# Decode attention with a gated side branch on one core: the last output weights in six pieces, the result in four stores

## The chip, the core and the metric

The kernel runs on one core of a Trainium2 chip. The metric is the device time of one execution in microseconds (us), the median of several runs. The core has a matrix engine (PE, with its weight loads as PEld), VectorE (DVE), ScalarE (ACT), GpSimd (POOL) and SyncE (SP). SP and ACT each issue transfers on a queue of their own; all transfers share 16 DMA engines. In the traces q1 is SP's queue and q10 is ACT's.

## The reference

One decode step for 8 sequences: layer norm of x, attention over the last 2048 keys of a cache with 8 key heads and 32 query heads, the output projection, multiplied by the SiLU of a gated feed-forward branch, plus x.

```python
x  = A_x                                   # 8 x 1 x 512
xn = _layernorm(x, axis=-1)
# _A_ref, with W = 2048, Hq = 32, Hkv = 8, Dh = 128
q = (xn @ wq).reshape(B, 1, 32, 128).transpose(0, 2, 1, 3)
k = jnp.repeat(k_cache[:, :, Sk - W:, :], 4, axis=1)
v = jnp.repeat(v_cache[:, :, Sk - W:, :], 4, axis=1)
p = softmax(einsum("bhqd,bhkd->bhqk", q, k) * 128 ** -0.5)
o = einsum("bhqk,bhkd->bhqd", p, v)
s = o.transpose(0, 2, 1, 3).reshape(B, 1, 4096) @ wo      # wo: 4096 x 512
# _B_ref
h = sigmoid(xn @ w_gate) * (xn @ w_up)
g = silu(h @ w_down)
return x + s * g                            # 8 x 1 x 512, bf16
```

Keys and values that are read are 32 MB each, the weights some 13 MB; the result is 8 KB.

## The kernel before, in words

Everything comes in through SP's queue (`q0`), but for half of `w_gate` and one small copy of x, which ACT's queue (`q1`) takes. The loads stand in one list in the order in which they are wanted (`later`, line 107). A load goes out when its buffer pool has room: there are five buffers for keys ("k") and four for values ("v"), of 2 MB each, and `pump` (line 110) issues from the head of the list only, so an entry that has no room holds back all behind it. `free` (line 116) is called where the program has used up a buffer. An issue then waits on SP for the last reader of the buffer that it takes over.

The list is: x and the feed-forward weights in value buffers (three of them), the query weights in two key buffers, sixteen key tiles (sequence b, half i of the heads) with the value tiles three places behind, and at the end the output weights `wo` in pieces (line 176, `want_rows` at 120, `load_rows` at 97). Each partition holds 32 rows of `wo` of 1 KB; a piece is rows t0 to t1 of every partition, in one buffer of a pool.

For each sequence PE turns the keys (line 421), multiplies them with the queries (440), and two sequences behind multiplies the probabilities with the values (537, in `values`, which frees a value tile after its last column). The order of the last two sequences is written out by hand from line 627 on. Then come the output products: rows 0 to 19 (`KS` is 20) of `wo` into `part_ps` (line 659), copied by ACT (669); this partial sum (line 685) and the rows 20 to 31 one by one go into `fin_ps`, four products per row at four column blocks (673, called at 686).

`fin_ps` has the four blocks of 128 output columns on partitions 0, 32, 64 and 96 and, within a block, the eight sequences four partitions apart (`Z` is 32, `S` is 4, `NB` is 4). VectorE multiplies by the gate (`prod`, line 688) and adds x (`y_bf`, line 690). Two stores write the result (line 693), one on each queue, two blocks each. x in the same layout is `x4_sb`, called x_sb in the trace; ACT loads it at line 157.

Of the kernel before, what the change touches and what calls it, by code (L numbers as in the profile page):

```python
# [10 lines left out]
def kernel(  # L11
# [14 lines left out]
    P = 128  # L26
# [54 lines left out]
    q0, q1 = nc.sync, nc.scalar  # L81
# [15 lines left out]
    def load_rows(w, tag, per, r0, r1, name):  # L97
        t = pools[tag].tile([P, r1 - r0, w.shape[1]], bf16, name=name, tag=tag)
        q0.dma_start(  # L99
            out=t[:], in_=w.rearrange("(p r) n -> p r n", r=per)[:, r0:r1, :]  # L100
        )
        return t
# [4 lines left out]
    def later(tag, f):  # L107
        todo.append((tag, f))

    def pump():  # L110
        while todo and room[todo[0][0]] > 0:
            tag, f = todo.pop(0)
            room[tag] -= 1
            f()
# [5 lines left out]
    def want_rows(name, w, tag, per, r0, r1):  # L120
        def f():
            t = load_rows(w, tag, per, r0, r1, name)
            for r in range(r0, r1):
                weights[(name, r)] = t[:, r - r0, :]

        later(tag, f)

    def want_cache(tiles, cache, tag, b, i):
        def f():
            tiles[(b, i)] = load_cache(cache, tag, b, i)  # L130

        later(tag, f)

    RT = 32
    KS = 20
# [4 lines left out]
    Z = 32  # L140
    S = Z // B
    NB = D // P
# [28 lines left out]
    for n in range(len(order) + AHEAD):  # L171
        if n < len(order):
            want_cache(k_tiles, A_k_cache, "k", *order[n])
        if n >= AHEAD:
            want_cache(v_tiles, A_v_cache, "v", *order[n - AHEAD])
    for t0, t1 in ((0, 12), (12, KS), (KS, 26), (26, 30), (30, RT)):
        want_rows("wo_sb", A_wo, "k", RT, t0, t1)

    pump()

# [7 lines left out]
        out=perm[:].rearrange("k (l p) -> k l p", l=G),  # L188
        in_=ident[:].rearrange("k (p l) -> k l p", l=G),
# [13 lines left out]
        out=rstd[:], in_=mv[:, 1:2], func=AF.Sqrt, bias=eps_t[:], scale=1.0  # L203
# [4 lines left out]
        out=xn_bf[:],  # L208
# [8 lines left out]
    for kt in range(KT):  # L217
        nc.tensor.transpose(  # L218
            out=xnT_ps[:, kt, :],
            in_=xn_bf[:].rearrange("b (p kt) -> b kt p", kt=KT)[:, kt, :],  # L220
# [11 lines left out]
    for t in p_buf:  # L232
# [7 lines left out]
        out=own_q[:], in_=ident_f[:].rearrange("k (h q) -> k q h", q=NDQ), axis=AX.X  # L240
# [3 lines left out]
        out=sel_z[:], in_=ident_f[:].rearrange("k (j z) -> k z j", z=Z), axis=AX.X  # L244
# [6 lines left out]
    def hidden(name):  # L251
# [21 lines left out]
        out=h_sb[:].rearrange("k t p -> k p t"),  # L273
# [7 lines left out]
        out=hT_sb[:].rearrange("k t z -> k (t z)"),  # L281
        in_=h_sb[:].rearrange("k t p -> k (t p)"),
# [4 lines left out]
    for t in range(FT):  # L287
        j = t % NB
# [53 lines left out]
    for x in range(Hkv // JQ):  # L342
        for r in range(rep):
            nc.tensor.transpose(
                out=qT_ps[:, x, r, :], in_=q_bf[:, x, r, :], identity=ident[:]
            )
        nc.vector.tensor_copy(
            out=qm_sb[:, :, x * JQ : (x + 1) * JQ, M0 : M0 + rep],
            in_=qT_ps[:, x].rearrange("d r (j z) -> d z j r", z=Z)[:, ::S],
# [11 lines left out]
    for i in range(NQ):  # L361
        nc.vector.tensor_copy(
            out=turn_rows[:].rearrange("k (i j l r) -> k i j l r", i=NQ, j=NJ, l=G)[
                :, i
            ],
            in_=ident[:].rearrange("k (l j i r) -> k i j l r", i=NQ, j=NJ, l=G)[:, i],
        )
        nc.vector.reduce_sum(
            out=sel_den[:, i * Hh : (i + 1) * Hh].rearrange("k (l r) -> k l r", l=G),
            in_=ident_f[:].rearrange("k (l j i r) -> k i l r j", l=G, j=NJ, i=NQ)[:, i],  # L370
            axis=AX.X,
        )
    for e in range(2):
        nc.vector.reduce_sum(
            out=sel_out[:, e, :].rearrange("k (i h) -> k i h", i=NQ),
            in_=ident_f[:].rearrange(
                "k (i m e h) -> k e i h m", i=NQ, m=NJ // 2, e=2
            )[:, e],
# [9 lines left out]
        out=sel_res[:],  # L388
# [6 lines left out]
        out=sel_sum[:], in_=sel_den[:].unsqueeze(2).to_broadcast([P, Hq, NDQ])  # L395
# [261 lines left out]
    for t in range(KS):  # L657
        j = t % NB
# [29 lines left out]
    nc.vector.tensor_tensor(out=prod[:], in0=gg_sb[:], in1=fin_ps[:], op=ALU.mult)  # L688
    y_bf = work.tile([P, P], bf16, name="y_bf")
    nc.vector.tensor_tensor(out=y_bf[:], in0=prod[:], in1=x4_sb[:], op=ALU.add)  # L690
    HP = P // 2
    for x, q in enumerate((q0, q1)):
        q.dma_start(
            out=out.flatten_outer_dims().rearrange("b (j c) -> j b c", c=P)[
                x * NB // 2 : (x + 1) * NB // 2
            ],
            in_=y_bf[x * HP : (x + 1) * HP : S, :],
        )


# [28 lines left out]
```

## Time and profile before

| | us |
|---|---|
| median of three runs (199.91 to 200.09) | 200.05 |
| the profiled execution | 200.05 |
| its span, first to last instruction | 198.1 |
| PE busy in the span | 153.7 |
| VectorE busy | 121.6 |
| ScalarE busy | 37.6 |
| last load landed, PE resumes | 194.02 |
| `y_bf` done, stores issued | 195.12 |
| mean transfer rate over the span | 411 GB/s, 81.32 MB |

The page cuts the span into 40 slices of about 5 us; a digit is the busy share of a slice in tenths, and "GB/s" what the transfer engines moved in it. The part on queues gives packets, megabytes and the share of the 16 engines' time. The chain of work that ended last is followed back from the last instruction and lists start, duration and what ran. The timeline merges like instructions of one engine: start, duration, engine, line, operation, and in brackets how long the engine had been idle and what ended that. Windows give, for a stretch, its length, the busy time and count of PE, PEld, DVE, ACT and POOL, the clock granted to PE, the share of the transfer engines and GB/s. The granted clock is 1.00 up to 191 us, 0.88 in the us from 191 and 0.50 from 192 on.

Besides these views I use the trace's records of single packets (start, duration, size, queue), which no view lists; where a number is from them it is said.

### The profile page before, as it was taken

The numbers are of one execution on the slowest core, as the hardware profiler recorded it, in microseconds if no ns is written. First come the engines' busy times: TensorE is split into PE (matmuls) and PEld (weight loads), VectorE is DVE, ScalarE is ACT, GpSimd is POOL, SyncE is SP. The second block draws the span as 40 slices with busy tenths as digits, with TensorE's granted clock in tenths as the row PEclk, the third lists the DMA queues.
The fourth block names the chain that finished last, engine by engine and source line by source line (L and its number), as shares of the span: only waits on it lengthen the run. The fifth ranks groups of instructions, "written<-read, shape, count | busy, mean of one in ns | idle before, by whom it ended". The sixth has DMA issues, their size and how long they took to land.

```text
span 198.1 us, 4749 instructions
## 1 busy us (share of the span) xinstructions
PE 153.7 (78%) x2128; PEld 103.8 (52%) x2128; DVE 121.6 (61%) x225; ACT 37.6 (19%) x91; POOL 1.4 (1%) x10
## 2 busy tenths in 40 slices
PE   0435365999799996979798959997989797888652
PEld 0101125776676574656565646675657565566421
DVE  3752025999798586748675927587858674752301
ACT  3301010001700500230024000600140033082010
POOL 2000000000000000000000000000000000000000
PEclk9999999999999999999999978999999999999985
DMA  6999999999999999999999999999999999999970
GB/s 225 436 428 430 440 430 427 430 424 428 424 447 427 424 424 427 427 430 440 430 430 422 427 427 430 433 428 437 424 424 424 433 433 427 437 420 432 410 314 14
DMA packets 6299, 81.32 MB, mean 411 GB/s; under 512 B 768, under 2 KB 776, under 8 KB 1416
## 3 DMA queue, kind: packets, MB, share of 16 engines
q1 hardware_dynamic: 6082, 80.10, 94.9%
q10 hardware_dynamic: 198, 0.93, 1.4%
q8 instruction: 16, 0.26, 0.5%
q14 instruction: 3, 0.02, 0.0%
HBM read 81.02 MB, written 0.01 MB: 409 GB/s over the span
## 4 chain that ended last, share of the span: by engine, by line
DMA 76%; PE 21%; SPq 1%; issue 0%; DVE 0%
DMA k_sb<-in_A_k_cache_dram 63%; PE kT_ps L421 12%; DMA wo_sb<-in_A_wo_dram 11%; PE o_ps L537 4%; PE s_ps L440 3%; DMA wg_sb<-in_B_w_gate_dram 2%; SPq L99 1%; PE fin_ps L673 1%; PE pT_ps L511 0%; DVE prod L688 0%; PE m_ps L475 0%; DVE y_bf L690 0%; PE m_ps L458 0%; SPq L89 0%
## 5 line engine op out<-in xcount | busy, mean ns | idle before, releaser
L426 DVE COPY kT_sb<-kT_ps 128x1024 bf16<-128x1024 bf16 x128 | 85.4, 688 | 35.7 <-PE kT_ps L421 34.9
L421 PE MATMUL kT_ps<-perm,k_sb 128*128 128x128 bf16 x1024 | 76.9, 224 | 15.0 <-DMA k_sb<-in_A_k_cache_dram 15.0
L421 PEld LDWEIGHTS <-k_sb 128*128 128x128 bf16 x1024 | 60.1, 100 | 35.2 <-DMA k_sb<-in_A_k_cache_dram 18.1
L537 PE MATMUL o_ps<-v_sb,pT_sb 128*32 128x256 bf16 x512 | 40.0, 278 | 1.2 <-DVE o_sb L558 0.9
L537 PEld LDWEIGHTS <-pT_sb 128*32 128x32 bf16 x512 | 22.1, 97 | 9.8 <-issue 3.3
L440 PE MATMUL s_ps<-kT_sb,qm_sb 128*32 128x512 bf16 x256 | 25.8, 393 | 0.7 <-DVE kT_sb L426 0.7
L488 ACT ACTIVATE p_buf<-s_ps,nb 32x512 bf16<-32x512 f32 x32 | 21.7, 678 | 0.5
L481 ACT COPY nb<-m_ps 128x1 f32<-128x1 f32 x8 | 1.3, 159 | 91.7 <-PE m_ps L475 91.7
L511 PE MATMUL pT_ps<-turn_rows,p_buf 128*128 128x128 bf16 x128 | 11.0, 230 | 1.5 <-ACT p_buf L488 1.5
L504 DVE COPY pT_sb<-pT_ps 128x1024 bf16<-128x1024 bf16 x14 | 9.6, 687 | 3.9 <-PE pT_ps L511 3.9
L511 PEld LDWEIGHTS <-p_buf 128*128 128x128 bf16 x128 | 9.4, 151 | 3.4 <-ACT p_buf L488 2.1
L440 PEld LDWEIGHTS <-qm_sb 128*32 128x32 bf16 x256 | 6.6, 93 | 7.7 <-issue 1.2
L553 ACT ACTIVATE o_odd<-o_ps,own_col 128x128 f32<-128x128 f32 x8 | 2.9, 368 | 29.0 <-PE o_ps L537 29.0
L325 PE MATMUL q_ps<-wq_sb,xnT_sb 128*32 128x512 bf16 x32 | 3.8, 627 | 4.2 <-DMA wq_sb<-in_A_wq_dram 4.2
L488 ACT ACTIVATION_READ_ACCUMULATOR p_buf<-s_ps,nb 32x1 f32 x32 | 5.9, 184 | 0.0
L455 DVE TENSOR_REDUCE st<-s_ps 128x1 f32<-128x512 f32 x8 | 5.5, 684 | 0.5 <-PE s_ps L440 0.5
L341 DVE CAST q_bf<-q_ps 128x512 bf16<-128x512 f32 x1 | 0.7, 692 | 7.4 <-PE q_ps L325 7.4
L218 PE MATMUL xnT_ps<-ident,xn_bf 8*128 8x8 bf16 x4 | 0.3, 174 | 5.6 <-DVE xn_bf L207 5.6
L580 DVE SCALAR_TENSOR_TENSOR own<-m_ps,inv,own_q 128x128 f32<-128x128 f32 x8 | 2.8, 344 | 3.1 <-PE m_ps L571 3.1
L558 DVE SCALAR_TENSOR_TENSOR o_sb<-o_ps,own_col,o_odd 128x128 f32<-128x128 f32 x8 | 2.7, 340 | 3.1 <-ACT o_odd L553 3.1
L325 PEld LDWEIGHTS <-xnT_sb 128*32 128x32 bf16 x32 | 1.1, 130 | 6.4 <-issue 4.7
L255 PE MATMUL h_ps<-wu_sb,xnT_sb 128*32 128x448 bf16 x16 | 1.7, 572 | 3.3 <-DMA wu_sb<-in_B_w_up_dram 3.3
(72 smaller groups left out, 58.3 us busy)
## 6 DMA issues: line engine op xcount, KB each, us to landing
k_sb<-in_A_k_cache_dram SPq DMA_DIRECT2D x16, 2048.0 KB, 33.4
v_sb<-in_A_v_cache_dram SPq DMA_DIRECT2D x16, 2048.0 KB, 27.1
wq_sb<-in_A_wq_dram SPq DMA_DIRECT2D x2, 2048.0 KB, 22.4
wu_sb<-in_B_w_up_dram SPq DMA_DIRECT2D x1, 1792.0 KB, 10.1
wd_sb<-in_B_w_down_dram SPq DMA_DIRECT2D x1, 1792.0 KB
wo_sb<-in_A_wo_dram SPq DMA_DIRECT2D x1, 1536.0 KB, 18.2
wo_sb<-in_A_wo_dram SPq DMA_DIRECT2D x1, 1024.0 KB
wg_sb<-in_B_w_gate_dram ACTq DMA_DIRECT2D x1, 896.0 KB, 4.6
```

The costliest lines, as they stand in the source:

```text
L325: nc.tensor.matmul(q_ps[x][Z * j : Z * (j + 1), :], lhsT=xnT_sb[:, kt, :], rhs=weights[("wq_sb", kt)][:, g * rep * Dh : (g + 1) * rep * Dh ...
L421: nc.tensor.transpose(out=kT_ps[:, c, :], in_=k_sb[:, j * CU + h * CH + c, :], identity=perm[:],)
L426: nc.vector.tensor_copy(out=kT[(b, u)][:, h * CH : (h + 1) * CH, :], in_=kT_ps[:])
L440: nc.tensor.matmul(s_ps[b][NR * l : NR * (l + 1), :], lhsT=qm_sb[:, b, i * G + l, o : o + Z], rhs=t[:, :, PG * l : PG * (l + 1)], start=(u ...
L455: nc.vector.reduce_max(out=st[b][:], in_=s_ps[b][:], axis=AX.X)
L488: nc.scalar.activation(out=p_buf[b % 2][rows, :, l, :], in_=s[rows, :].rearrange("k (c p) -> k p c", p=PG), func=AF.Exp, bias=nb[rows, :], ...
L504: copy(out=pT[b][:, h * CH : (h + 1) * CH, :], in_=pT_ps.pop(h)[:])
L511: nc.tensor.transpose(out=pT_ps[h][:, c, :], in_=p_buf[b % 2][:, :, :, h * CH + c].rearrange("k p l -> k (p l)"), identity=turn_rows[:],)
L537: nc.tensor.matmul(o_ps[rows, b % 2, :].rearrange("k (e d) -> k e d", e=2), lhsT=pT[b][:, c, rows], rhs=v[:, m, c], start=(c == 0), stop=( ...
L553: nc.scalar.mul(out=o_odd[:], in_=o_ps[:, b % 2, Dh:], mul=own_col[:, 1:2])
L558: nc.vector.scalar_tensor_tensor(out=o_of[b // 2][:, b % 2, :], in0=o_ps[:, b % 2, :Dh], scalar=own_col[:, 0:1], in1=o_odd[:], op0=ALU.mul ...
L580: nc.vector.scalar_tensor_tensor(out=own[:], in0=m_ps[:, b % 2, P : 2 * P].rearrange("p (q t) -> p q t", q=NDQ), scalar=inv[y][:, b % 2 : ...
```

## The change

Two places. The rows 20 to 31 of `wo` came in pieces of 6, 4 and 2 rows; they now come in pieces of 5, 4, 2 and 1, and the last one asks for a value buffer where the others ask for key buffers. The result was stored by one transfer of two blocks on each queue; now each block of eight rows is a transfer, blocks 0 and 2 on SP and 1 and 3 on ACT.

```diff
-    for t0, t1 in ((0, 12), (12, KS), (KS, 26), (26, 30), (30, RT)):
+    for t0, t1 in ((0, 12), (12, KS), (KS, 25), (25, 29), (29, 31)):
         want_rows("wo_sb", A_wo, "k", RT, t0, t1)
+    want_rows("wo_sb", A_wo, "v", RT, 31, RT)
```

```diff
-    HP = P // 2
-    for x, q in enumerate((q0, q1)):
-        q.dma_start(
-            out=out.flatten_outer_dims().rearrange("b (j c) -> j b c", c=P)[
-                x * NB // 2 : (x + 1) * NB // 2
-            ],
-            in_=y_bf[x * HP : (x + 1) * HP : S, :],
-        )
+    y = out.flatten_outer_dims().rearrange("b (j c) -> j b c", c=P)
+    for j in range(NB):
+        q = (q0, q1)[j % 2]
+        q.dma_start(out=y[j], in_=y_bf[Z * j : Z * (j + 1) : S, :])
```

## The prediction

> **What bounds the kernel now.** I read the page's forty slices first, then the chain of work that ended last, then the end in order of time, because the change touches only the last transfers in and the transfers out. From the page:
>
> ```profile
> DMA  6999999999999999999999999999999999999970
> GB/s 225 436 428 430 440 430 427 430 424 428 424 447 427 424 424 427 427 430 440 430 430 422 427 427 430 433 428 437 424 424 424 433 433 427 437 420 432 410 314 14
> q1 hardware_dynamic: 6082, 80.10, 94.9%
> q10 hardware_dynamic: 198, 0.93, 1.4%
> ```
>
> Apart from the first slice the transfer engines are full until some 190 us, at 410 to 447 GB/s. The bytes are the bound; the change moves the same bytes in, so only what happens around the last of them can move the time. The chain from 185 us on:
>
> ```profile
> 171.27 22.10 DMA wo_sb<-in_A_wo_dram
> 193.37 0.04 issue
> 193.41 1.04 PE fin_ps L673 x24
> 194.45 0.02 issue
> 194.47 0.30 DVE prod L688
> 194.77 0.03 issue
> 194.80 0.29 DVE y_bf L690
> ```
>
> The landing of the last output weights ends last; then come matrix products, two VectorE operations (over at 195.09) and, behind the chain, the stores. The timeline of that stretch:
>
> ```profile
> 192.17 0.83 PE L673 MATMUL fin_ps<-wo_sb,oP_sb 128*32 128x128 bf16 x24
> 193.41 1.02 PE L673 MATMUL fin_ps<-wo_sb,oP_sb 128*32 128x128 bf16 x24 [0.41 <-DMA wo_sb<-in_A_wo_dram]
> 194.02 0.14 PEld L673 LDWEIGHTS <-oP_sb 128*32 128x32 bf16 x7 [0.19 <-issue]
> 195.12 0.65 SPq L693 DMA_DIRECT2D out_dram<-y_bf  x1
> 195.12 0.61 ACTq L693 DMA_DIRECT2D out_dram<-y_bf  x1
> ```
>
> Six rows (24 products) were there at 192.17. At 193.41 PE resumes with the four rows 26 to 29, and the weight load that resumes at 194.02 belongs to rows 30 and 31, the last piece. Both stores are issued at 195.12, 0.65 us on SP and 0.61 on ACT. When they moved shows in narrow windows (the columns end with the DMA share and GB/s):
>
> ```profile
> 196.36:196.52 0.16, 0.00 (x0) 0.00 (x0) 0.00 (x0) 0.00 (x0) 0.00 (x0) 0.50 0.12 26
> 196.52:196.72 0.20, 0.00 (x0) 0.00 (x0) 0.00 (x0) 0.00 (x0) 0.00 (x0) 0.50 0.00 0
> 196.72:196.88 0.16, 0.00 (x0) 0.00 (x0) 0.00 (x0) 0.00 (x0) 0.00 (x0) 0.50 0.12 26
> ```
>
> Two bursts: by the packet records ACT's (196.37 to 196.50), then SP's (196.73 to 196.86), each at a share of 0.12, that is about 2 of 16 engines. SP sees SP's completion at 197.20; the closing barrier ends the span at 198.08. So from the stores' issue at 195.12 the path is SP's: issue 0.65, flight to the first packet 0.96, packets 0.13, completion 0.34, sum 2.08.
>
> **The last rows, 12-8-6-4-2 to 12-8-5-4-2-1.** The last piece shrinks from two rows to one, so one row's four products fewer follow the last landing. The six rows at 192.17 took 0.83 us, one product 0.31 (median for line 673), so a row adds (0.83 - 0.31) / 5 = 0.10. Saved: 0.10 us. Against it, the packets: in the packet records one of 6, 4, 2 and 1 KB takes 234, 159, 84 and 44 ns (the last in the load of x), a completion 9; 5 KB lies halfway between 4 and 6, 197. An engine moves eight packets per piece. Before: 8 x (234 + 159 + 84) + 3 x 9 = 3843 ns; after: 8 x (197 + 159 + 84 + 44) + 4 x 9 = 3908. The last landing is 0.07 us later. Together -0.03; bounds -0.10 (more packets cost nothing) and +0.07 (PE gains nothing). The middle pieces land 8 x 37 = 296 ns earlier, worth nothing: their products were never last.
>
> The one-row piece needs a value buffer. Nineteen tiles went through that pool (three weights, sixteen cache tiles) and it has four buffers, so this one takes the place of value tile (6, 0). Its last reader is among the first 16 of the 32 products that start at 176.29 and take 1.51, thus free at about 177.05. SP holds the transfer from 172.18 (end of the fifth issue) until then; behind it on SP there are only the stores, at 195. An issue of 0.44 makes it 177.5, while the same queue works off what it has until past 190. Cost nothing, covered by some 13 us; were the release later than that, each us would show fully. Transfers also take turns at eight completion semaphores and wait for the previous holder (SP's store waited for a cache tile from 172.2 to 179.4, far ahead of need). The new piece takes that of a cache tile issued at 150.05; two of the four stores take those of the first two output pieces, of which the second was in use at 190.35. None of these waits is late.
>
> **Four stores.** Now each store names two blocks of eight rows, later one block. q10's 198 packets are 144 for half of w_gate (128 data and 16 completions), 36 for x in four blocks (32 and 4) and 18 for its store: 16 data, 2 completions, two engines. The load of x_bf, eight rows of 1 KB with one level, appears as 8 data and 8 completions. So I expect 16 packets per new store on eight engines, q10 at 198 - 18 + 32 = 212, q1 at 6082 + 144 - 18 + 32 = 6240. The Trainium skill, "DMA: Bandwidth & Descriptors", section "Why a DMA increments its semaphore by 16 and not by 1", has it that the engine count is the largest up to 16 that divides both sides' slowest dimensions, two now and eight afterwards; this trace agrees for the two.
>
> Issue: the next rows are
>
> ```profile
> 0.73 0.41 SPq L149 DMA_DIRECT2D x_bf<-in_A_x_dram  x1
> L99 SPq DMA_DIRECT2D wo_sb<-in_A_wo_dram x5: 376/436/586, 169.7 to 171.8; - x5
> 1.17 1.18 ACTq L157 DMA_DIRECT2D x_sb<-in_A_x_dram  x1
> ```
>
> The first is the eight-row shape, 0.41; the second is issues in a row (median 0.44, some 0.04 apart). I take 0.41 + 0.04 + 0.44 = 0.89 where 0.65 stood: +0.24. Low bound twice 0.376, +0.14; high bound, two at today's 0.65, +0.69. The third line is a far row, ACT's x in blocks at 1.18: as the second issue it would make +0.98.
>
> Flight: ACT's 0.63 and SP's 0.96 differ although they were issued together; x_bf took 0.55. A last SP store that again races one of ACT's is nearest to SP's row: 0.96, change 0. Low bound 0.55, -0.41; the trace shows no longer one on empty engines. Packets: one data and one completion per engine, 18 + 9 ns, instead of eight and one: 0.13 to 0.03, -0.10. Completion 0.34, unchanged.
>
> **Sum.** -0.03 + 0.24 + 0 - 0.10 = +0.11. The profiled execution took 200.05 (span 198.1 and 1.95 around it), which is also the median of the three runs; so 200.16, I say 200.15. What a measurement of this kernel can tell from no change is about 0.2%, 0.4 us, and this is inside.
>
> **Rivals.** *Dear issues (slower).* On SP and ACT, between y_bf at 195.09 and the last store's flight: if an issue's price belongs to a transfer behind a wait and not to its shape, both cost 0.65, +0.69 - 0.10 - 0.03 = +0.56, 200.6. It decides from 0.57 us per issue (2 x 0.57 + 0.04 - 0.65 = 0.53, less 0.13 is 0.40). For it: 0.65 and 0.61 are the only stores there are, and ACT's 1.18. Against it: 0.41 for eight plain rows, and the fifth output piece, which also waited, at 0.38.
>
> *Shorter flight (faster).* Eight engines with one packet each instead of two shared engines with eight: SP's 0.33 over ACT is queueing on these two engines and goes. Then the flight is 0.55 and the sum +0.24 - 0.41 - 0.10 - 0.03 = -0.30, 199.75; with the cheapest issues -0.40, 199.65. For it: SP's burst starts 0.23 us after ACT's ends, at the same two engines' share. Against it: the new stores of both queues share engines as well.
>
> *Stores in sequence (slower).* The second store on a queue moves only after the first has landed: 0.41 + twice (0.96 + 0.03 + 0.34) = 3.07 against 2.08, so +0.99 - 0.03, 201.0. Against it: the output pieces were issued 0.49 us apart and the engines stayed full. The Trainium skill, same page, section "Rules for kernel authors", advises against splitting into disjoint partition halves because "they serialize", and for merging small transfers; the loads here show no gap between transfers, and no row has two stores on one queue.
>
> That the pieces do nothing (their gain and loss cancel) is what the sum says already.
>
> **Chances.** Forecast 0.52 (own range 199.8 to 200.45), dear issues 0.24, shorter flight 0.19, in sequence 0.05. Over 0.4 us slower: 0.03 of the first, 0.19 of the second, all 0.05 of the last, 0.27. Over 0.4 faster: 0.02 of the first and 0.11 of the third (its cheap end and a completion that shortens too), 0.13. The rest, 0.60, is within. The range goes from 199.5, under the shorter flight, to 200.8, over dear issues; the sequence and the far row of 1.18 stay outside.
>
> **What would show it.** Right: each store's issue near 0.41 to 0.45, two in a row on SP and ACT; the first weight load of row 31 some 0.07 later than 194.02 and prod near 194.44; last completion seen about 0.1 us later, counted from y_bf. Wrong: issues of 0.57 or more; store packets less than 0.6 us behind the last issue; the one-row piece issued after 190; a gap in the DMA share before 190, or a last landing moved by more than 0.2 us, which would say that something besides the end has changed.

## The result and the profile after

The changed kernel takes 200.87 us (median of 6 runs, 200.80 to 200.94), the kernel before 200.01 (6 runs beside it, 199.91 to 200.09). The medians differ by 0.86 us, 0.43%; the ratio estimated from all these runs is 1.0038, 95% interval 1.0028 to 1.0049, so the change is slower. The profiled execution took 200.82 with a span of 199.01; before it was 200.05 and 198.08. The loss is inside the span: it grew by 0.93, and the time outside it shrank by 0.16.

From the page of the changed kernel, the transfer share in forty slices and the two queues:

```profile
DMA  6999999999999999999999999999999999999960
q1 hardware_dynamic: 6240, 80.10, 94.5%
q10 hardware_dynamic: 212, 0.93, 1.4%
```

The stream is as full as before. The packet counts are 6240 and 212, so every store now has eight data packets and eight completions, one of each for every one of eight engines. The chain of work that ended last, from 192 us on:

```profile
192.12 0.04 issue
192.16 1.63 PE fin_ps L674 x44
193.79 0.01 issue
193.79 0.64 PE fin_ps L674 x12
194.43 0.02 issue
194.46 0.30 DVE prod L689
194.75 0.02 issue
194.78 0.29 DVE y_bf L691
```

`y_bf` is ready at 195.07 here and was at 195.09 before. PE works from 192.16 on without a long gap here: by the trace's clock records its granted clock fell to 0.50 at 188.66 already, against 191.76 before, so it is behind with the earlier rows. The last row still waits for its weights. By the semaphore and instruction records its piece has landed at 194.07 (the last piece before: 193.98), and its first product begins at 194.11. So up to the stores nothing is lost. The timeline behind it:

```profile
195.10 1.59 SPq L695 DMA_DIRECT2D out_dram<-y_bf  x2
195.10 1.40 ACTq L695 DMA_DIRECT2D out_dram<-y_bf  x2
```

SP is busy issuing for 1.59 us where it was 0.65. By the list of the result's transfers (minimum, median and maximum in ns, then first and last start) each issue is dear:

```profile
L695 SPq DMA_DIRECT2D out_dram<-y_bf x2: 766/769/772, 195.1 to 195.9; - x2
L695 ACTq DMA_DIRECT2D out_dram<-y_bf x2: 648/681/714, 195.1 to 195.9; - x2
```

In the list of line 721, the end of the program, one of SP's closing checks waits 1.16 us; it is the one for the last store:

```profile
L721 SPq EVENT_SEMAPHORE  x8: 17/28/1161, 196.7 to 199.0; - x8
```

Windows over the four bursts of packets (the last two columns are the share of the transfer engines and GB/s):

```profile
196.44:196.55 0.11, 0.00 (x0) 0.00 (x0) 0.00 (x0) 0.00 (x0) 0.00 (x0) 0.50 0.12 19
196.55:196.80 0.25, 0.00 (x0) 0.00 (x0) 0.00 (x0) 0.00 (x0) 0.00 (x0) 0.50 0.00 0
196.80:196.90 0.10, 0.00 (x0) 0.00 (x0) 0.00 (x0) 0.00 (x0) 0.00 (x0) 0.50 0.14 21
196.90:197.17 0.27, 0.00 (x0) 0.00 (x0) 0.00 (x0) 0.00 (x0) 0.00 (x0) 0.50 0.00 0
197.17:197.27 0.10, 0.00 (x0) 0.00 (x0) 0.00 (x0) 0.00 (x0) 0.00 (x0) 0.50 0.14 21
197.27:197.52 0.25, 0.00 (x0) 0.00 (x0) 0.00 (x0) 0.00 (x0) 0.00 (x0) 0.50 0.00 0
197.52:197.62 0.10, 0.00 (x0) 0.00 (x0) 0.00 (x0) 0.00 (x0) 0.00 (x0) 0.50 0.14 21
```

ACT, SP, ACT, SP, one burst every 0.36 us; the last ends at 197.62, before it was 196.86. Step by step on SP, from the instruction and packet records:

| us | before | after | difference | predicted |
|---|---|---|---|---|
| stores issued at | 195.12 | 195.10 | -0.02 | -0.03 |
| issue on SP | 0.65 | 1.59 | +0.94 | +0.24 |
| flight of the last store to its first packet | 0.96 | 0.85 | -0.12 | 0 |
| its packets | 0.13 | 0.09 | -0.05 | -0.10 |
| to the completion seen | 0.34 | 0.34 | 0 | 0 |
| then to the end of the checks | 0.13 | 0.29 | +0.17 | (none) |

The sum is +0.92; the span grew by 0.93.

The last row is small and was not foreseen. At the end SP checks the semaphores in six steps, the first for one semaphore and the others for two, about 0.06 us apart when nothing is waited for. Before, the last store's semaphore stood in the fifth step. Now the last store holds the semaphore of the second output piece, which stands in the second step: four more checks follow it.

### The profile page after: what moved, and what is told of

Read it like the earlier page. It is cut to its first block, busy times and chain, and to the rows that moved or that the text cites. A ratio compares the mean times of both kernels' runs of the same rounds, so it can differ in the third digit from the quotient of the medians.

```text
span 199.0 us, 4753 instructions
## 1 busy us (share of the span) xinstructions
PE 154.6 (78%) x2128; PEld 104.2 (52%) x2128; DVE 121.7 (61%) x225; ACT 37.7 (19%) x91; POOL 1.4 (1%) x10
## 3 DMA queue, kind: packets, MB, share of 16 engines
q1 hardware_dynamic: 6240, 80.10, 94.5%
## 4 chain that ended last, share of the span: by engine, by line
DMA 75%; PE 22%; issue 0%; SPq 0%; ACT 0%; DVE 0%
DMA k_sb<-in_A_k_cache_dram 62%; PE kT_ps L422 12%; DMA wo_sb<-in_A_wo_dram 10%; PE o_ps L538 4%; PE s_ps L441 3%; DMA wg_sb<-in_B_w_gate_dram 2%; PE fin_ps L674 1%; PE part_ps L660 1%; PE pT_ps L512 0%; ACT part L670 0%; SPq L99 0%; DVE prod L689 0%; PE m_ps L476 0%; DVE y_bf L691 0%; PE m_ps L459 0%
```

## The experiments

Every kernel below keeps what is not shown in its diff. "Tail" is from the stores' issue to the end of the span of the profiled execution: 2.96 us before, 3.92 in the changed kernel. Interval means 95%.

**e1: the pieces alone.** The changed kernel with

```diff
-    y = out.flatten_outer_dims().rearrange("b (j c) -> j b c", c=P)
-    for j in range(NB):
-        q = (q0, q1)[j % 2]
-        q.dma_start(out=y[j], in_=y_bf[Z * j : Z * (j + 1) : S, :])
+    HP = P // 2
+    for x, q in enumerate((q0, q1)):
+        q.dma_start(
+            out=out.flatten_outer_dims().rearrange("b (j c) -> j b c", c=P)[
+                x * NB // 2 : (x + 1) * NB // 2
+            ],
+            in_=y_bf[x * HP : (x + 1) * HP : S, :],
+        )
```

> The six pieces of wo, with the two stores of the kernel before. Theory (the loss is all in the stores; the pieces are neutral): y_bf is done within 0.1 us of the kernel before (195.1), the time is 199.9 to 200.1, ratio 0.999 to 1.001. Rival (the one-row piece delays the end, and the stores cost less than they seem): 200.3 or more, and the last landing more than 0.2 us later.

Measured: 199.80 (11 runs) beside 200.08 (27), ratio 0.9982, interval 0.9973 to 0.9991. Stores issued at 195.16, tail 2.92. The rival falls; the pieces are no loss and came out 0.10 us better than the theory's range.

**e2: the four stores alone.** The kernel before, with the lines marked - above in place of those marked +.

> The four stores, with the five pieces of wo of the kernel before. Theory (issues of 0.77 us, two in a row on SP): 200.8 to 201.0, the whole loss of 0.9 us, with two issues of 0.7 to 0.8 us on SP. The final checks of the completion semaphores may come 0.06 us cheaper than in the changed kernel, since the last store holds another semaphore. Rival (pieces and stores share the loss): 200.3 to 200.6.

Measured: 200.91 (5 runs) beside 200.08, ratio 1.0040, interval 1.0027 to 1.0052; stores issued at 195.19, tail 3.86. The stores carry the whole loss: 0.83 us here, 0.86 with the pieces. The tail is 0.06 under the changed kernel's, as expected from the place of the semaphore: three checks follow instead of four.

**e4: neighbouring partitions.** What is stored is not the result.

```diff
-        q.dma_start(out=y[j], in_=y_bf[Z * j : Z * (j + 1) : S, :])
+        q.dma_start(out=y[j], in_=y_bf[Z * j : Z * j + B, :])
```

> The changed kernel, but each store takes eight neighbouring partitions (32j to 32j+7) in place of eight that lie four apart; what is stored is therefore not the result. Theory A (the dear issue comes from the partition step of four, which the load of x_bf at 0.41 us does not have): issues of 0.40 to 0.45, time about 200.87 - 2 x 0.33 = 200.2. Theory B (it comes from something else: the direction, or both queues issuing at once): issues stay at 0.65 to 0.77, time 200.8 to 200.9.

The stores of this kernel:

```profile
L695 SPq DMA_DIRECT2D out_dram<-y_bf x2: 298/308/317, 195.2 to 195.5; - x2
L695 ACTq DMA_DIRECT2D out_dram<-y_bf x2: 347/354/360, 195.2 to 195.6; - x2
```

The windows over its first pair of bursts:

```profile
195.95:196.00 0.05, 0.00 (x0) 0.00 (x0) 0.00 (x0) 0.00 (x0) 0.00 (x0) 0.50 0.23 36
196.05:196.10 0.05, 0.00 (x0) 0.00 (x0) 0.00 (x0) 0.00 (x0) 0.00 (x0) 0.50 0.24 36
```

Measured: 199.76 (10 runs) beside 200.08, ratio 0.9984, interval 0.9975 to 0.9993; tail 2.79. The number of rows, the bytes, the number of engines, the direction and the place in the program are the same, and an issue takes 0.30 to 0.36 us instead of 0.65 to 0.77. Theory A holds, and the gain is larger than it said, because the flight is shorter too: SP's last store has its first packet 0.47 us after its issue instead of 0.85, and the two queues' bursts are 0.10 us apart instead of 0.36.

**e7: SP alone.** Blocks 1 and 3 are not stored.

```diff
-    for j in range(NB):
-        q = (q0, q1)[j % 2]
+    for j in (0, 2):
+        q = q0
```

> The changed kernel, but blocks 1 and 3 of the result are not stored: SP issues its two stores, ACT none. Theory A (SP and ACT slow each other's issues and flights): two issues of 0.4 to 0.5 us and a flight of 0.55 to 0.63 instead of 0.85, time 200.87 - 0.6 - 0.2 = 200.0 to 200.1. Theory B (the price is the store's own): issues still 0.7 to 0.8, and only the flight is shorter by 0.2 to 0.3, time 200.5 to 200.7.

```profile
L695 SPq DMA_DIRECT2D out_dram<-y_bf x2: 687/728/769, 195.1 to 195.9; - x2
```

Measured: 200.36 (10 runs) beside 200.08, ratio 1.0015, interval 1.0006 to 1.0024; tail 3.39. With nothing on ACT the issues cost 0.77 and 0.69, so the price is the store's own: theory B. Both flights are 0.63 now, 0.22 less than the last store's in the changed kernel. The second issue is 0.08 shorter, and the checks give 0.22, since the last store's semaphore is in the last step.

**e9: a step of two.** What is stored is not the result.

```diff
-        q.dma_start(out=y[j], in_=y_bf[Z * j : Z * (j + 1) : S, :])
+        q.dma_start(out=y[j], in_=y_bf[Z * j : Z * j + 2 * B : 2, :])
```

> The changed kernel, but each store takes eight partitions two apart in place of four apart, so that what is stored is not the result. Theory A (any gap between partitions makes the issue dear): issues of 0.65 to 0.77 us as with step four. Theory B (the price grows with the step): 0.45 to 0.55, between step one (0.30 to 0.36) and step four.

```profile
L695 SPq DMA_DIRECT2D out_dram<-y_bf x2: 772/772/773, 195.2 to 196.1; - x2
L695 ACTq DMA_DIRECT2D out_dram<-y_bf x2: 648/686/725, 195.2 to 196.0; - x2
```

Measured: 200.97 (one run), tail 3.93. Theory A: step two costs what step four costs, 0.77 on SP; no other step was tried.

**e8: the second transfer is a load.** Blocks 2 and 3 are not stored; eight rows of x go into a scratch tile instead, which nothing reads.

```diff
+    xb = A_x.flatten_outer_dims().rearrange("b (j c) -> j b c", c=P)
+    back = work.tile([P, P], bf16, name="back")
     for j in range(NB):
         q = (q0, q1)[j % 2]
-        q.dma_start(out=y[j], in_=y_bf[Z * j : Z * (j + 1) : S, :])
+        rows = slice(Z * j, Z * (j + 1), S)
+        if j < 2:
+            q.dma_start(out=y[j], in_=y_bf[rows, :])
+        else:
+            q.dma_start(out=back[rows, :], in_=xb[j])
```

> The changed kernel, but the second transfer on each queue is a load of eight rows of x into partitions four apart in place of the store of blocks 2 and 3, which are not stored. Theory A (the step is the price, whichever the direction): the loads' issues take 0.65 to 0.77 us. Theory B (only stores are dear): 0.35 to 0.45.

```profile
L701 ACTq DMA_DIRECT2D back<-in_A_x_dram x1: 651/651/651, 196.1 to 196.1; - x1
L701 SPq DMA_DIRECT2D back<-in_A_x_dram x1: 773/773/773, 196.2 to 196.2; - x1
```

Measured: 201.40 (one run). Theory A: a load into partitions four apart is as dear to issue as a store from them.

**e5: one store of all 32 rows.** On top of e1:

```diff
-    HP = P // 2
-    for x, q in enumerate((q0, q1)):
...
+    q0.dma_start(
+        out=out.flatten_outer_dims().rearrange("b (j c) -> j b c", c=P),
+        in_=y_bf[::S, :],
+    )
```

> The six pieces, and one store of all 32 rows (partitions four apart) on SP, none on ACT. Theory (an issue's price grows with the rows that lie four apart: 8 rows 0.77, 16 rows 0.65, the load of 32 rows 1.18, and the engines used matter too): an issue of 1.0 to 1.3 us, a flight of 0.63 since nothing races it, time 199.8 + 0.45 - 0.33 = 199.9 to 200.1. Rival (a flat price per transfer): an issue of 0.65, time 199.8 - 0.33 = 199.5.

```profile
L692 SPq DMA_DIRECT2D out_dram<-y_bf x1: 673/673/673, 195.2 to 195.2; - x1
```

Measured: 199.73 (10 runs) beside 200.18 (21), ratio 0.9980, interval 0.9971 to 0.9989; tail 2.72. The theory that the price grows with the rows falls: 8, 16 and 32 rows with gaps cost 0.77, 0.65 and 0.67 on SP. It is nearly flat per transfer, as the rival said, though the number of engines changes along with the rows (8, 2 and 4 by the packet counts). The time lies between the two forecasts: the flight is 0.63 as expected, but the packets take 0.04 longer than in e1 and one more check follows the store. The load of x in blocks, 1.11 to 1.18 on ACT and also with a step of four, is dearer for a reason that no run isolates.

**n1: the layout mended.** The eight sequences on neighbouring partitions of each block of 32, and the true result stored:

```diff
-    S = Z // B
...
-        q1.dma_start(
-            out=x4_sb[::S, :],
-            in_=A_x.flatten_outer_dims().rearrange("b (j c) -> j b c", c=P),
-        )
+        xb = A_x.flatten_outer_dims().rearrange("b (j c) -> j b c", c=P)
+        for j in range(NB):
+            q1.dma_start(out=x4_sb[Z * j : Z * j + B, :], in_=xb[j])
...
-    nc.vector.tensor_copy(out=xnT_sb[:, :, ::S], in_=xnT_ps[:])
+    nc.vector.tensor_copy(out=xnT_sb[:, :, :B], in_=xnT_ps[:])
...
-            in_=qT_ps[:, x].rearrange("d r (j z) -> d z j r", z=Z)[:, ::S],
+            in_=qT_ps[:, x].rearrange("d r (j z) -> d z j r", z=Z)[:, :B],
...
-                    out=oP_sb[:, :, S * b],
+                    out=oP_sb[:, :, b],
...
-        q.dma_start(out=y[j], in_=y_bf[Z * j : Z * (j + 1) : S, :])
+        q.dma_start(out=y[j], in_=y_bf[Z * j : Z * j + B, :])
```

> The changed kernel with the eight sequences on neighbouring partitions of each block of 32 everywhere (x, queries, output columns, result), so that the four stores read neighbouring partitions and x in blocks comes in four loads. Theory (the partition step is the price of the issue): issues of 0.30 to 0.36 us as in e4, time 199.6 to 199.9, faster than the kernel before and about 1.1 us faster than the changed one. Rival (the other places pay for the new layout): above 200.0. The four loads of x on ACT should cost 0.35 us each where the one load with step four took 1.18.

Its stores, its loads of x in blocks, and from the timeline two early issues on SP:

```profile
L693 SPq DMA_DIRECT2D out_dram<-y_bf x2: 302/308/313, 195.5 to 195.9; - x2
L693 ACTq DMA_DIRECT2D out_dram<-y_bf x2: 303/306/309, 195.5 to 195.9; - x2
```

```profile
L158 ACTq DMA_DIRECT2D x_sb<-in_A_x_dram x4: 278/464/594, 1.2 to 2.7; - x4
```

```profile
1.59 0.43 SPq L99 DMA_DIRECT2D wu_sb<-in_B_w_up_dram  x1
5.92 0.33 SPq L99 DMA_DIRECT2D wd_sb<-in_B_w_down_dram  x1
```

Measured: 200.01 (11 runs) beside 200.18, ratio 0.9993, interval 0.9984 to 1.0002, so no faster than the kernel before by what can be told. The stores do what the theory says: issues of 0.31, tail 2.83. The loads of x took 0.28 to 0.59 each, not the 0.35 expected. But they are issued at 195.54, 0.44 later than in the changed kernel, and that gives the gain back: the rival is half right. Three more loads at the start move every transfer to another completion semaphore; the load of `w_down` then waits for that of an earlier transfer and goes out at 5.92 instead of 2.08. That this is what makes the end later was not tested.

**s1 to s4: the parts side by side on one chip.** The changed kernel, e1, e2 and e5 again, five rounds each.

> The changed kernel again, on one chip with the three that follow, so that the two parts of the change can be told apart without a change of chip. Theory (the stores cost 0.9 us, the pieces save 0.0 to 0.15): 0.8 to 0.9 us over the kernel before. Rival (the pieces save 0.3, as the ratio of e1 has it): 0.6 to 0.7 over it.

> e1 again, the six pieces with the two old stores. Theory: 0.0 to 0.15 us under the kernel before on the same chip. Rival: 0.3 under it.

> e2 again, the four stores with the five old pieces. Theory: 0.9 us over the kernel before, and 0.0 to 0.15 over s1. Rival: 0.3 over s1.

> e5 again, the six pieces with one store of 32 rows on SP. Theory (a transfer with gaps between its partitions pays about 0.65 us to issue however many rows it has, and one alone has a flight of 0.63 in place of 0.96): 0.2 us under s2 and 0.2 to 0.4 under the kernel before. Rival (e5 was fast by chance of its chip): equal to s2.

| kernel | us (median) | ratio to before, interval | stores issued at | tail |
|---|---|---|---|---|
| before (21 runs) | 200.06 | | | |
| s1, changed | 200.83 | 1.0040 (1.0026 to 1.0053) | 195.03 | 3.94 |
| s2, pieces | 199.73 | 0.9985 (0.9976 to 0.9993) | 195.08 | 2.91 |
| s3, four stores | 200.96 | 1.0041 (1.0029 to 1.0054) | 195.23 | 3.86 |
| s4, pieces and one store | 199.59 | 0.9978 (0.9969 to 0.9987) | 195.09 | 2.72 |

The four stores cost 0.90 (s3) and 1.10 (s1 over s2). Under the same stores the pieces save 0.13 (s3 to s1, as the theory has it) and 0.33 (before to s2, as the rival has it), and s1, at 0.77 over the kernel before, lies between theory and rival, so the size of this small gain stays open. What is seen of it: over all profiles with the old layout the stores are issued at 195.15 on average with six pieces (ten profiles) and 195.18 with five (three), but the ten alone run from 195.03 to 195.33, so these 0.03 us can't be told from nothing; with two stores, the sixth piece also moves SP's store to the last step of the checks, 0.05 in the tail; and the time outside the span is about 1.80 with six pieces, 1.86 with five pieces and four stores, and 1.90 to 1.95 in the kernel before, for which no trace shows a cause. s4 is faster than both kernels, 0.47 us under the one before (0.2 to 0.4 was expected) and 1.24 under the changed one, and 0.14 under s2 where 0.2 was expected.

## Why the prediction was right, and where it was wrong

The direction of the sum (+0.11, slower) held, its size did not: 200.15 was forecast and 200.87 measured, over the forecast's own range and 0.07 over the wide one. "Within 0.2%" had the largest chance, 0.60, and over 0.4 us slower 0.27; the change is +0.38% by the ratio and +0.43% by the medians. The forecast of +0.11 was itself within what the prediction said could not be told from no change, so that its sign came true is little merit. The rival of dear issues (200.6, chance 0.24) is what happened, beyond its own price, and the prediction's own sign of being wrong, "issues of 0.57 or more", is what the trace shows.

*The pieces: right up to the stores.* Row 31's first product was expected 0.07 after 194.02 and came at 194.11; the last weights landed 0.09 later, and the four products fewer made up for it, so `y_bf` was done 0.02 earlier in the changed kernel's profile, where 0.03 was expected. What the pieces save in the whole time, 0.13 to 0.33, is more than this and was not foreseen; most of its cause stays open. The value buffer cost nothing: the one-row piece was issued at 177.20, against "free at about 177.05".

*The store's shape: right.* The packets came out exactly as counted, 6240 and 212. The Trainium skill's rule for the number of engines ("DMA: Bandwidth & Descriptors", section "Why a DMA increments its semaphore by 16 and not by 1") gave eight, and this trace has eight data packets and eight completions per store.

*The issue: wrong, and the failed step.* The prediction took "0.41 + 0.04 + 0.44 = 0.89", from the load of x_bf and the output pieces, and measured is 0.77 + 0.05 + 0.77 = 1.59. It matched the load of x_bf by its number of rows and by having one level, and the pieces as issues in a row, and both address neighbouring partitions. The stores address every fourth. e4 closes the gap by the step alone; e9, e8 and e7 exclude, for steps of two and four, the width of the step, the direction and the other queue. Why a gap costs the queue's engine this time, no run shows. The row of the right kind was in the prediction: the load of x in blocks, with the same step of four, put aside as far, and the old store itself. The stated rival gave as its reason that the price belongs to "a transfer behind a wait"; the second store waits for nothing late and costs as much, and in e4 the first stores wait for the same `y_bf` and cost half, so its price was near and its reason wrong.

*The flight: nearly right.* 0.96 was kept and 0.85 measured; e7 gives 0.63 for a store that races none. So the rival of the shorter flight falls: with eight engines instead of two, SP's first store still has its first packet 0.95 behind its issue, and one that races none has 0.63 on eight engines (e7) as on four (e5). The packets were put at 0.03, as if the eight engines started together, and took 0.09: by the packet records a store's first and last packet start 0.08 apart.

*Stores in sequence: this rival falls.* SP's second issue begins at 195.92, before a packet of the first has moved (196.81). In e7 the second burst starts 0.74 us after the first, the distance between the ends of the two issues, and has the same flight of 0.63; in e4 SP's second burst starts 0.27 after its first has ended, less than the 0.34 that a completion takes. The Trainium skill's "they serialize" ("DMA: Bandwidth & Descriptors", section "Rules for kernel authors"), for which the page gives the sharing of the engines as its reason, is not seen as a wait for the landing. Another sentence of the same page, section "Issuing engines are not separate DMA queues", calls the issue's time "usually small relative to the DMA itself". Here the last store's issue takes 0.77 us, its packets 0.09, and the way from the end of its issue to its completion seen 1.28, so for such small stores with gaps the issue is no small part.

*Not in the sum:* the place of the last store's semaphore in the closing checks, +0.17. Moving the semaphore by itself was not tried; e2 and e7 move it along with other things and show tails that fit.

## What to carry to other kernels

A price for issuing a transfer is to be taken from a row with the same partition step, not only the same size: the small stores here cost 0.30 to 0.36 us with neighbouring partitions and 0.60 to 0.78 with gaps, for 8, 16 or 32 rows. The step is not all that counts: the load of `w_down`, which takes all partitions, was issued in 0.72 us in the kernel before and in 0.33 in n1, for a reason that no run isolates. At the end of this kernel nothing hides the issue, so the stores with gaps did best as one transfer (tail 2.72), and four stores of neighbouring partitions came close to it (2.79 and 2.83); one store of neighbouring partitions was not tried. One more transfer also shifts which completion semaphore each later transfer takes, and with it early waits and the closing checks.

## What the runs showed of the hardware beyond that

Two queues that issue stores with gaps at the same time don't send at the same time: the bursts of SP and ACT start 0.36 us apart, with 16 rows on two engines (before) and with 8 on eight (after) alike. With neighbouring partitions, on eight engines each as well, they start 0.10 apart in e4 and 0.02 in n1, where by the packet records the two bursts overlap (196.33 to 196.42 and 196.35 to 196.44). So it isn't the number of engines that keeps them apart. A common stage that prepares one transfer after the other, and takes longer over one with gaps, would fit, but that was only argued.
